# Holding score runs at the head of a query block for the 64-row key tile

## The chip, the cores and the metric

The kernel runs on one core of a Trainium2 chip. The metric is the device time of one execution in microseconds (us). Ten executions of the kernel before were timed; their median is 1172.02 us.

## What is computed

For each of 8 batches, with sequence length S = 3008, width 256 and 64 columns in z:

```
scores = (1/S) * z @ z.T
attn   = max(scores, 0) ** 2
x      = u * (attn @ v)
h      = max(x.T @ w_tok1, 0) @ w_tok2          # mixes tokens, 256 inner
y      = x + h.T
out    = y + max(y @ w_ch1, 0) @ w_ch2          # mixes channels, 1536 inner
```

The scores of a batch are symmetric, because both sides are z.

## The kernel before

**Tiles.** The 3008 tokens are cut into 6 query blocks of 512 (the last has 448) and 24 key tiles of 128 rows, four to a group; group g has the tokens of block g. The last key tile has only 64 rows. Batches, blocks and groups are counted from 0, and "block (4, 5)" is block 5 of batch 4.

**Scores.** A score unit is two key tiles against one query block. z has 64 columns, so a score matmul uses 64 rows of TensorE's array. z is stored twice, in rows 0 to 63 and 64 to 127, and the two matmuls of a unit (L399) use one half each and run side by side. ScalarE takes the ReLU out of PSUM (L437, L425), VectorE squares in place (L445, L473). From batch 1 on only blocks with g >= q are scored. A block g > q is turned by a transposing DMA from SP (`flip`, L492), giving tile `fl`, and serves again as block (g, q). A block with g = q is a triangle tile: only the upper part is scored, and three small transposes on SP (`flip_tiles`, L485) fill in the rest; the first two follow its first unit, the third its second unit. Up to three units are scored in one run, one for each free slot of a ring of three PSUM slots that the mixer also uses.

**Attention times v.** For each query block, six groups of key tiles are multiplied with v into two accumulators, one for each half of the 256 columns (`av_matmul`, L533). These matmuls use 128 rows. The last key tile has 64 rows; its two matmuls, one for each accumulator and again one on each half of the array, are the pair that `do_tails` issues (L533, shown as 64*128). The pair needs the block of the last group (LAST = 5) to be ready and both accumulators to be free. The accumulators become free when VectorE has multiplied the previous block's by u (`gate`, L628 and L633). For query block 5 the block of the last group is the triangle tile (5, 5).

**Mixer.** When a batch's attention is done, its token and channel matmuls (L675, L692, L729, L771, all with 128 rows) are put in two lists, from which pieces are taken between the attention matmuls of the next batch. The transposes of x (L640) and of the sum (L708) and the output's stores (L788, L804) are issued by SP too, as are those of u (L189) and z (L126). GpSimd (POOL) issues the loads of z, v and u (L113, L168, L171, L179), each attached to a step of the attention groups.

**Order.** The kernel writes its own order of instructions, by a planner that runs while the kernel is built. It keeps a clock `pe[0]` for TensorE, estimated times at which engines and tiles are ready, and adds 0.095 us whenever TensorE goes between 64-row and 128-row matmuls (`on_pe`). In each step it picks "scores" (a run of score units), "av" (half a group of attention times v) or "mixer" (a piece of the mixer). `n_now` is the number of units that could be scored at once, `ts` the time when their slots are free, `whole` says that a full run is at hand, `lead` is the number of attention tiles that are alive and `low` that these are at most 3. `blk` is the current query block: `blk.slot` counts the groups it has begun, `blk.tails` says that its pair is issued. `tails_ready` is the time when the pair can be issued. A score run takes the pair along when it can be issued by then; otherwise the pair is issued at the latest before the block's last group:

```python
        if pick == "scores":
            if blk is not None and tails_ready(blk) <= t + 0.3:
                do_tails(blk, max(t, tails_ready(blk)))
            score_run(units[done_units:done_units + n_now], max(pe[0], ts))
```

```python
            if final and not blk.tails:
                do_tails(blk, max(start, tails_ready(blk)))
```

Of the kernel before, what the change touches and what calls it, by code (L numbers as in the profile page):

```python
# [53 lines left out]
def kernel(  # L54
# [12 lines left out]
    B, S, D = u.shape  # L67
# [9 lines left out]
    NQ = (S + QW - 1) // QW  # L77
    NG = KT // GK
# [74 lines left out]
    def fill(n, tag="ps", bufs=3):  # L153

        wp = psum.tile([P, QW], F32, tag=tag, name="wp", bufs=bufs)
        for _ in range(n):
            nc.tensor.matmul(
                wp[:], zero[:, :P], zero[:], start=True, stop=True, skip_group_check=True)
# [94 lines left out]
    LAST = NG - 1  # L253
# [40 lines left out]
    FAR = 1e9  # L294
# [11 lines left out]
    def next_op():  # L306
        best = None
        for e, ops in waiting.items():
            for op in ops:
                if has_room(op.room):  # L310
                    key = (max(free[e], op.ready), -op.first, op.ready)
                    if best is None or key < best[0]:
                        best = (key, e, op)
        return best

    def run_engines(until):

        while True:
            best = next_op()
            if best is None or best[0][0] > until:  # L320
                return
            (start, _, _), e, op = best
            waiting[e].remove(op)
            extra = shared(start, op.busy) - op.busy if e == "sp" else 0.0
            free[e] = start + op.busy + extra
            op.done.t = start + op.lat + extra
            op.fn(op.done.t)

    def known(*events):
        return max((FAR if d.t is None else d.t for d in events), default=0.0)  # L330
# [38 lines left out]
    def can_score(first_unit, most):  # L369

        n, at = 0, live["at"]
        for (b, q, g), pr in units[first_unit:first_unit + most]:
            if (b, q) not in turned or (b, g) not in turned:
                break
            at += pr == 0
            if at > ROOM["at"]:
                break
            n += 1
        return n
# [165 lines left out]
    def block_ready(blk, g):  # L545
        e = blocks.get((blk.b, blk.q, g))
        return FAR if e is None else known(e[0])

    def tails_ready(blk):

        if blk.tails:
            return FAR
        return max(block_ready(blk, LAST), known(*acc_free))

    def do_tails(blk, start):
        on_pe(start, "half", column_time(blk.W))
        blk.parts.setdefault(LAST, 2)
        for dh in range(DT):
            av_matmul(blk, LAST, GK - 1, dh, False)
        blk.tails = True  # L560
        finished(blk, LAST)

    def next_half(t):

        blk = cur[0]
        if blk is None:
            return FAR, None
        if blk.g is not None:
            dh, tiles = blk.steps[blk.half]
            events = early.get((blk.b, blk.q, blk.g), [])[tiles[0]:tiles[-1] + 1]  # L570
            return max(t, known(acc_free[dh], *events)), blk.g
        at = max(t, known(acc_free[0]))
        ready = [(block_ready(blk, g), i) for i, g in enumerate(blk.todo)]
        soon = [i for r, i in ready if r <= at + 0.05]
        if soon:
            return at, blk.todo[soon[0]]
        r, i = min(ready)
        return max(at, r), blk.todo[i]
# [275 lines left out]
    def next_piece(t):  # L854

        best = FAR, None
        slots = [d.t for d in ring if d.t is not None]
        if opened[0] is not None:
            lists = [opened[0]] + [l for l in (heads, tails) if l is not opened[0]]
        else:  # L860
            lists = [heads, tails]
        for l in lists:
            if not l:
                continue
            p = l[0]
            if p.opens and not p.closes and opened[0] is not None:
                continue
            r = max(t, known(*p.needs))
            if p.room and not has_room(p.room):
                r = FAR  # L870
            if not p.closes:
                r = max(r, min(slots)) if slots else FAR
            if r < FAR and r <= t + 0.05:
                return r, l
            if r < best[0]:
                best = r, l
        return best

    def do_piece(start, l):
        p = l.pop(0)  # L880
        start, end = on_pe(start, "full", p.cost)
        opened[0] = l if p.opens else None if p.closes else opened[0]
        p.fn(end)
# [114 lines left out]
    NOW = 0.05  # L998
    STARVED = 0.7
    while cur[0] is not None or heads or tails:  # L1000
        run_engines(pe[0])
        t = pe[0]
        ta, g = next_half(t)
        tm, pieces = next_piece(t)
        blk = cur[0]

        def has_turned(us):
            return known(*(turned[b, c] for (b, q, g_), _ in us for c in (q, g_)))


        n = can_score(done_units, RING)
        slots = sorted(d.t for d in ring if d.t is not None)
        n_now = min(n, len(slots))
        ts = FAR
        if n_now:
            at = max(t, has_turned(units[done_units:done_units + n_now]))
            ts = max([at] + [slots[i] - 0.1 - 0.216 * i for i in range(n_now)])
            new = sum(pr == 0 for _, pr in units[done_units:done_units + n_now])
            if new:
                ts = max(ts, sorted(at_free)[new - 1] - 0.6)  # L1020
        lead = live["at"]
        whole = n_now == RING or (n_now and done_units + n_now == len(units))
        low = lead <= 3
        hold = n >= RING and lead <= 4


        now = sum(d <= t + NOW for d in slots[:n_now])
        left = sum(op.busy for op in waiting["act"])
        starved = blk is not None and blk.b + blk.q == 0 and (
            max(free["act"], t) + left < t + STARVED)  # L1030

        pick = None
        if n_now and ts <= t + NOW and (whole or (low and n_now >= 2)):
            pick = "scores"
        elif (starved and now and can_score(done_units, now) == now
              and has_turned(units[done_units:done_units + now]) <= t + NOW):
            pick, n_now, ts = "scores", now, t
        elif hold and opened[0] is not None and tm <= t + NOW and pieces is opened[0]:
            pick = "mixer"
        elif hold and ta <= t + NOW:  # L1040
            pick = "av"
        elif budget > 0 and tm <= t + NOW:
            pick = "mixer"
        elif ta <= t + NOW:
            pick = "av"
        elif tm <= t + NOW and (budget > -5.0 or blk is None):
            pick = "mixer"
        else:
            options = [(ta, "av"), (tm, "mixer")]
            if n_now and (whole or low):  # L1050
                options.append((ts, "scores"))
            when, what = min(options)
            op = next_op()
            if op is not None and op[0][0] <= when:
                run_engines(op[0][0])
                continue
            assert when < FAR, "nothing can run"
            if blk is not None and blk.b == 0 and blk.q == 0 and blk.acc[1] is None:
                idle = int((when - t) / 0.22)
                if idle:  # L1060
                    fill(idle, "acc1", 1)
            pick = what
# [5 lines that stand above are left out]
            done_units += n_now  # L1068
        elif pick == "av":
            step = (blk.b * NQ + blk.q) * NG + blk.slot  # L1070
            if blk.g is None:
                for f in fetch.get(step, []):
                    f()
            do_half(ta, g)
        else:
            budget -= pieces[0].cost
            do_piece(tm, pieces)
        if pick != "mixer" and blk is not None and blk.b >= 1:
            budget += per_batch * (pe[0] - t) / flat
# [31 lines left out]
```

## Time and profile before

| what | value |
|---|---|
| median of ten executions | 1172.02 us (1170.40 to 1180.49) |
| the profiled execution: its time, its span | 1180.49 us, 1178.4 us |
| TensorE matmuls (PE): busy, instructions | 1162.4 us, 7049 |
| VectorE (DVE), ScalarE (ACT), GpSimd (POOL): busy | 541.6, 521.5, 161.0 us |
| score matmuls L399: instructions | 732 |
| pairs of the 64-row key tile, L533 | 48 pairs |
| transposes L485 into `at`: issues, median to landing | 123, 2.4 us |
| transposes L492 into `fl`: issues, median to landing | 105, 4.0 us |
| DMA engines: mean rate | 141 GB/s |

The profile is of one execution on the chip. A time is counted from the start of the span. "PE" is TensorE's matmuls and "PEld" its weight loads, which overlap. A matmul's busy time goes on after the next one has started, so the time that a matmul costs is read from start to start. A line "X <- Y" among the waits gives the idle time of X that ended with Y, then how often and the longest. "SPq" is SP's queue of issues; for a DMA the time from issue to landing is given apart.

### The profile page before, as it was taken

To read this page: it belongs to the slowest core of one execution; us is meant where nothing else is said; L and a number is where in the kernel's file an instruction comes from. 1 tells how busy PE (TensorE), PEld (TensorE's weight loads), DVE (VectorE), ACT (ScalarE), POOL (GpSimd) and SP (SyncE) were. 2 spreads that over 40 slices of the span, in tenths; PEclk is the share of its full clock that TensorE was granted. 3 is DMA by queue.
4 is the path that set the end of the run, shared out by engine and by line. 5 is a ranking of instruction groups with operands and counts; after the bars stand their busy time and mean duration, and the time that the engine had idled before them with its cause. 6 is when DMAs were issued, how large, how long until landed. Compare 5 with 4: busy or idle time off the path is not lost.

```text
span 1178.4 us, 17791 instructions
## 1 busy us (share of the span) xinstructions
PE 1162.4 (99%) x7049; PEld 630.7 (54%) x7049; DVE 541.6 (46%) x819; ACT 521.5 (44%) x650; POOL 161.0 (14%) x328
## 2 busy tenths in 40 slices
PE   9997999999999999999999999999999999999998
PEld 3332455655556555465555555555554655555666
DVE  5684643436523464334634354342552436512544
ACT  7885542343633355334533436345353445513221
POOL 3471001012011110110201210011101010000000
PEclk9998999999999999999999999999999999999999
DMA  9999836896578984797859896697677978632121
GB/s 167 186 132 185 160 91 149 174 169 123 137 149 167 166 152 115 142 180 146 162 111 184 153 155 136 125 191 140 126 144 143 190 137 155 126 94 63 50 81 63
DMA packets 472883, 165.57 MB, mean 141 GB/s; under 512 B 436640, under 2 KB 450528, under 8 KB 472800
## 3 DMA queue, kind: packets, MB, share of 16 engines
q1 hardware_dynamic: 444944, 131.74, 54.2%
q0 software_dynamic: 27344, 32.32, 19.6%
q8 instruction: 55, 0.90, 0.3%
q10 hardware_dynamic: 512, 0.38, 0.1%
q14 instruction: 28, 0.23, 0.1%
HBM read 65.40 MB, written 24.64 MB: 76 GB/s over the span
## 4 chain that ended last, share of the span: by engine, by line
PE 95%; DMA 2%; DVE 1%; ACT 1%; issue 0%; POOL 0%; SPq 0%; ACTq 0%; DVEq 0%
PE acc L533 40%; PE op L771 21%; PE hp L729 21%; PE sc L399 6%; PE a_ps L675 4%; PE h_ps L692 3%; DMA fl<-at 1%; DMA ur<-in_u_dram 1%; ACT at L437 1%; DMA uT<-ur 0%; DMA zf<-in_z_dram 0%; DVE xT L698 0%; POOL v_sb L168 0%; DVE xT L628 0%; SPq L640 0%
## 5 line engine op out<-in xcount | busy, mean ns | idle before, releaser
L533 PEld LDWEIGHTS <-v_sb 128*128 128x128 bf16 (+1 forms) x2304 | 209.4, 98 | 267.3 <-issue 65.4
L533 PE MATMUL acc<-at,v_sb 128*128 128x512 bf16 (+3 forms) x1464 | 351.1, 379 | 1.3 <-DVE xT L628 0.7
L742 ACT ACTIVATE h2pre<-hp 128x1024 bf16<-128x1024 f32 (+1 forms) x191 | 191.1, 1006 | 364.4 <-PE hp L729 363.3
L437 ACT ACTIVATE at<-sc 128x1024 bf16<-128x1024 f32 (+1 forms) x284 | 271.9, 1023 | 167.6 <-PE sc L399 155.3
L445 DVE TENSOR_TENSOR at<-at 128x1024 bf16<-128x1024 bf16 (+1 forms) x284 | 200.5, 715 | 184.6 <-ACT at L437 184.3
L729 PE MATMUL hp<-xT,w_ch_sb 128*128 128x512 bf16 (+1 forms) x1152 | 266.7, 375 | 0.0
L771 PE MATMUL op<-w_ch_sb,h2pre 128*128 128x256 bf16 x2208 | 258.4, 273 | 0.3 <-DVE xT L698 0.2
L771 PEld LDWEIGHTS <-h2pre 128*128 128x128 bf16 x2208 | 216.0, 98 | 46.1 <-issue 0.5
L533 PE MATMUL acc<-fl,v_sb 128*128 128x512 bf16 (+1 forms) x840 | 199.9, 371 | 0.0
L729 PEld LDWEIGHTS <-w_ch_sb 128*128 128x128 bf16 x1152 | 112.7, 98 | 126.7 <-issue 0.2
L784 DVE TENSOR_TENSOR res<-op,u_sb 128x512 f32<-128x512 f32 x87 | 60.2, 692 | 206.4 <-PE op L771 206.4
L744 DVE TENSOR_SCALAR h2pre<-hp 128x1024 bf16<-128x1024 f32 (+1 forms) x97 | 117.3, 1209 | 52.1 <-PE hp L729 51.1
L628 DVE TENSOR_TENSOR xT<-acc,uT 128x512 bf16<-128x512 f32 (+1 forms) x96 | 63.3, 665 | 114.0 <-PE acc L533 113.6
L399 PE MATMUL sc<-zT 64*128 64x512 bf16 (+1 forms) x732 | 95.6, 361 | 0.5 <-ACT zT L986 0.2
L425 ACT ACTIVATE at<-sc 128x512 bf16<-128x512 f32 (+3 forms) x164 | 59.2, 445 | 67.7 <-PE sc L399 67.5
L125 POOL COPY zr<-zs 128x512 bf16<-128x512 bf16 x42 | 27.2, 648 | 400.7 <-DMA zT<-zr 395.6
L473 DVE TENSOR_TENSOR at<-at 128x512 bf16<-128x512 bf16 (+3 forms) x164 | 44.3, 324 | 59.1 <-ACT at L425 59.1
L399 PEld LDWEIGHTS <-zT 64*128 64x128 bf16 x732 | 31.3, 94 | 57.0 <-issue 40.1
L698 DVE TENSOR_TENSOR xT<-xT,h_ps 128x1024 bf16<-128x1024 bf16 (+1 forms) x48 | 55.7, 1192 | 6.3 <-PE h_ps L692 6.3
L675 PE MATMUL a_ps<-x_sb,w_tok_sb 128*128 128x256 bf16 x384 | 47.1, 281 | 7.6 <-ACT at L437 7.6
L675 PEld LDWEIGHTS <-w_tok_sb 128*128 128x128 bf16 x384 | 38.6, 101 | 17.1 <-issue 8.7
L168 POOL DMA_DIRECT2D v_sb<-in_v_dram x48 | 26.0, 547 | 145.1 <-PE acc L533 143.8
(43 smaller groups left out, 217.3 us busy)
## 6 DMA issues: line engine op xcount, KB each, us to landing
out_dram<-res SPq DMA_DIRECT2D x87, 256.0 KB, 2.2
v_sb<-in_v_dram POOLq DMA_DIRECT2D x40, 256.0 KB, 5.2
ur<-in_u_dram POOLq DMA_DIRECT2D x40, 256.0 KB, 5.4
zs<-in_z_dram POOLq DMA_DIRECT2D x35, 64.0 KB, 5.0
at<-at SPq DMA_TRANSPOSE x123, 2.4
fl<-at SPq DMA_TRANSPOSE x105, 4.0
v_sb<-in_v_dram POOLq DMA_DIRECT2D x8, 192.0 KB, 6.4
ur<-in_u_dram POOLq DMA_DIRECT2D x8, 192.0 KB, 5.7
```

Source lines behind the costliest of these rows:

```text
L399: nc.tensor.matmul(sc[:, r, c0:c1], zT[h, k * P:(k + 1) * P], zT[h, q * QW + c0:q * QW + c1], start=True, stop=True)
L425: nc.scalar.activation(a3[:, i, c0:c1], sc[:, r, c0:c1], ACT.Relu, scale=inv_S)
L437: nc.scalar.activation(view, sv, ACT.Relu, scale=inv_S)
L445: nc.vector.tensor_mul(view, view, view)
L533: nc.tensor.matmul(o, vs[blk.b, g][rows, i, dh * P:(dh + 1) * P], rhs, start=first, stop=stop, skip_group_check=True)
L628: nc.vector.tensor_mul(xT[:, dh, :full * P].rearrange("p (t s) -> p t s", s=P), acc[:, :full * P].rearrange("p (t s) -> p t s", s=P), uT[: ...
L675: nc.tensor.matmul(st["a_ps"][:, th, :], w_tok1_sb[:, k, th * P:(th + 1) * P], x[:, :, i, :], start=(k == 0 and th == 0), stop=(k == KT - ...
L729: nc.tensor.matmul(hp[:, r, :W], w_ch1_sb[:, dc, cc * P:(cc + 1) * P], xT[:, dc, :W], start=(dc == 0), stop=(dc == DT - 1))
L742: nc.scalar.activation(h2[:, :, :W], hp[:, :, :W], ACT.Relu)
L744: nc.vector.tensor_single_scalar(h2[:, :, :W], hp[:, :, :W], 0.0, AX.max)
L771: nc.tensor.matmul(op[:, i, :], h2, w_ch2_sb[:, cc, :], start=(cc == 0 and (i == 0 or apart)), stop=(cc == CHT - 1), skip_group_check=True)
L784: nc.vector.tensor_add(res.rearrange("p i (h d) -> p i h d", d=P), op.rearrange("p i (h d) -> p i h d", d=P), us[:, :, half * 2:half * 2 + ...
```

## The change

A condition `together` is added ahead of the choice, and a score run is not picked by the first rule while it holds. It can hold only in query blocks from 2 on and in batches before the last. It has two cases. In the first, the block has begun no group, its pair is not issued and can't be within 0.3 us, but the block of the last group is already planned. In the second, the current block is block 4, its pair is issued, it is in its last group, and more than three attention tiles are alive. While the condition holds, the planner picks attention or mixer work by its other rules.

```diff
         pick = None
-        if n_now and ts <= t + NOW and (whole or (low and n_now >= 2)):
+        together = blk is not None and blk.q > 1 and blk.b < B - 1 and (
+            not blk.tails and blk.slot == 0 and tails_ready(blk) > t + 0.3
+            and block_ready(blk, LAST) < FAR
+            or blk.tails and blk.q == NQ - 2 and blk.slot >= NG and lead > 3)
+        if n_now and not together and ts <= t + NOW and (whole or (low and n_now >= 2)):
             pick = "scores"
```

`block_ready` is the time when a block of attention is ready, and FAR if it isn't planned yet; NQ and NG are 6. Nothing else in the kernel is changed.

## The prediction

> **What bounds the kernel now.** The page first: busy time by engine, then the chain that ended last.
>
> ```profile
> PE 1162.4 (99%) x7049; PEld 630.7 (54%) x7049; DVE 541.6 (46%) x819; ACT 521.5 (44%) x650; POOL 161.0 (14%) x328
> PE 95%; DMA 2%; DVE 1%; ACT 1%; issue 0%; POOL 0%; SPq 0%; ACTq 0%; DVEq 0%
> ```
>
> TensorE is busy 99% and carries 95% of the chain; nothing else comes near. Its row of waits says how much of its time is waiting:
>
> ```profile
> PE a_ps L675 <- ACT at L437: 7.6, 1, 7.6
> ```
>
> That one wait, at 104.8 us, is nearly all of it; the same view over 200 to 1100 us is empty. So where the change acts, an edit counts only if it alters the time from one matmul to the next, or creates a wait. The timeline of TensorE shows that time (start, busy time, rows, shape, count):
>
> ```profile
> 337.67 1.67 PE L533 MATMUL acc<-fl,v_sb 128*128 128x512 bf16 x7
> 339.28 0.39 PE L533 MATMUL acc<-at,v_sb 64*128 64x512 bf16 x2
> 339.60 1.90 PE L533 MATMUL acc<-fl,v_sb 128*128 128x512 bf16 x8
> 341.34 1.03 PE L729 MATMUL hp<-xT,w_ch_sb 128*128 128x512 bf16 x4
> ```
>
> Read the starts, not the busy times, which overlap. Eight matmuls take 341.34 − 339.60 = 1.74, so 0.216 each with rounding. Seven should end at 337.67 + 1.51 = 339.18; the 64-row pair starts at 339.28, 0.10 late. The pair takes 0.32 to the next matmul, while two 64-row matmuls on opposite halves of the array run together for 0.223. So entering 64-row work costs about 0.10 and leaving it about 0.09: **0.19 per visit**, with no engine waited for. A pair that rides with scores pays neither:
>
> ```profile
> 625.00 0.39 PE L533 MATMUL acc<-at,v_sb 64*128 64x512 bf16 x2
> 625.22 0.43 PE L399 MATMUL sc<-zT 64*128 64x128 bf16 x4
> ```
>
> Here the scores follow 0.22 after the pair.
>
> [...] the clock granted between 104.5 and 125 us is 0.75.
>
> **The change part by part.** In the two built programs the order of TensorE's instructions is the same up to the score run at 211.1 us; the counts (7049 matmuls) are the same throughout. Nothing is added or removed; runs are regrouped.
>
> *Visits removed.* The program before has 140 stretches of 64-row matmuls, 13 of them a lone pair; the changed one has 131, with 4 lone pairs. Ten lone pairs go (in blocks 3 and 5 of several batches, both counted from 0), one comes (block 5 of batch 4). Net 9 × 0.19 = **−1.7 us**. It is on the path: TensorE does not wait there. The pair itself costs 0.22 in either place.
>
> *Score runs held.* They start later, behind attention or mixer matmuls already in the plan. Behind them wait, on ScalarE the ReLU (L425, L437), on VectorE the square (L473, L445), on SP the transposes (L485, L492). ScalarE and VectorE are busy 44% and 46%, so they catch up; TensorE works meanwhile on tiles already made. I cost this at nothing while such tiles last. If they run out, or its score slots are late, TensorE waits: at the turn from block to block I found no such wait before. Around the last batch the order shifts too: TensorE waits there 0.2 (L771 at 1107.79, for VectorE) and may wait once more: 0 to 0.4, taken as 0.
>
> *POOL and SP.* Loads are issued by POOL at steps of the attention groups, so they move with groups. SP issues the same transposes in a changed order. No queue gains an instruction: 0, unless a transpose becomes late.
>
> *A transpose that becomes urgent.* The pair of block 5 reads the last key tile, there a triangle tile completed by L485 transposes. Before, that pair came at the end of block 5, over 17 us after landing in every batch from 1 on. Now it comes at the head. From the pair of block 4 to that of block 5 the changed order leaves, in batches 5 and 6, 34 matmuls of 512 columns and 4 of 448 (34 × 0.216 + 4 × 0.189 = 8.1) and two 64-row stretches (about 0.8 each with their changes): 9.8 us. In that time the second half of the triangle tile must be scored, squared, transposed. On SP its last transpose stands behind x_sb and zT. Nothing before shows this wait; the nearest case is batch 4, whose last transpose also comes this late:
>
> ```profile
> 628.07 1.18 SPq L485 DMA_TRANSPOSE at<-at  x1
> DMA to landing us min/median/max: 5.5/5.5/5.5
> ```
>
> It lands at 633.6, that is 8.6 after the block-4 pair at 625.00. It would fit in 9.8. But the same turn is the time of the loads. The DMA view for 323 to 332 us, no loads, and then for 911 to 916.5, the turn to batch 7:
>
> ```profile
> q1 hardware_dynamic: 4204, 1.25, 56.4%
> x_sb<-xT SPq DMA_TRANSPOSE x1, 2.7
> at<-at SPq DMA_TRANSPOSE x3, 2.3
> ```
>
> ```profile
> q0 software_dynamic: 296, 0.54, 88.4%
> q1 hardware_dynamic: 828, 0.20, 42.9%
> x_sb<-xT SPq DMA_TRANSPOSE x1, 11.2
> at<-at SPq DMA_TRANSPOSE x1, 9.1
> ```
>
> Columns of q: packets, MB, share. With POOL's queue (q0) at 88%, SP's queue (q1) moves 828 packets in 5.5 us against 4204 in 9, and a 2.3 us transpose takes 9.1. SP issues it here:
>
> ```profile
> 914.30 7.08 SPq L485 DMA_TRANSPOSE at<-at  x3
> ```
>
> So it lands at 923.4, which is 13.4 after the block-4 pair at 910.0. Lateness per place is thus from 8.6 − 9.8 < 0, so nothing, to 13.4 − 9.8 = 3.6. A gain is excluded, for the pair had slack before. I take **1.5** at each of the two places, below the middle since one of the two observed ends gives nothing: +3.0. Batch 1 has 13.8 us between its pairs, and there the transposes landed at 211.8 against a pair at 198.9, 12.9: 0 to 0.5, taken as 0. Batches 2 and 3 have over 20 us from scoring the tile to the pair: 0.
>
> *Sum.* −1.7 + 3.0 = **+1.3**. The profiled execution took 1180.49 (span 1178.4, about 2.1 around it); it is the slowest of ten, with the wait at 104.8 that lies ahead of the change. Its sum is 1181.8. The median, 1172.02, differs by that early part, which the change leaves alone, so the same +1.3 gives **1173.3**.
>
> **The rivals.** *Slower: the late triangle tile decides.* Both places lose the full 3.6, batch 1 adds 0.5: 7.7 − 1.7 = +6.0, **1178.0**; a halved clock after a wait could add 1 or 2. It decides once these waits exceed 1.7 + 3.5 = 5.2 together. For it: the load bursts recur at each turn. Against: batch 4's 8.6, and x_sb lands at 2.7 when loads come a little later.
>
> *Faster: the wait that goes is another one.* The next batch's scores stand close to their transposes before: a zT transpose issued at 910.15 lands 4.8 later, 915.0, and the score run that follows starts at 916.10, 1.1 behind. At 346.5 plus 5.8 against 353.1 it is 0.8. In executions where these land later, TensorE waits; the median is 1.6 over the lowest (1170.4). Held scores give them time. If the triangle tile is in time as well: −1.7 − 1.6 = −3.3, and with the loss of an average execution, perhaps 2.5 in place of 1.6, −4.2, **1167.8**. Against: no such wait in the profiled execution.
>
> *The change does nothing:* the held runs cost what the visits save, 1172.0. The order of instructions speaks against that, since nine visits are gone.
>
> **How the numbers follow.** A measurement of this kernel can tell about 0.3%, 3.5 us, from no change. Small net effect (1169 to 1175.5, the visits and part of the waits, the do-nothing case within): 0.42, predicted time 1173.3. Slower rival: 0.36. Faster rival: 0.22. The likeliest case alone covers 1168.5 to 1175.5; since cases of both signs hold most of the chance, the range runs from 1167.3 to 1179.0, leaving out about one in ten at each end: the two full waits with a long halved clock above, both gains at once below.
>
> **What would show it.** Right: nine fewer stretches of 64-row matmuls, each 0.19; a wait "PE acc L533 <- DMA at<-at" at the turns of batches 5 and 6, none in 2 and 3; the transposes just ahead of it at 5 to 10 us to landing. Wrong: no DMA wait on TensorE after 200 us (then −1.7 alone, 1170.3), a wait over 4 us there or a granted clock below 1 after it (slower), or new waits of scores L399 for ScalarE, which would mean that held scores starve the planner's slots.

## The result, and the profile after

The changed kernel takes **1185.1 us** (median of 9 runs, 1183.12 to 1191.47) against 1171.52 us for the kernel before, timed on the same chip (32 runs). The ratio is 1.0105, with a 95% interval of 1.0082 to 1.0127: slower by about 1%, or 13.6 us. The prediction was 1173.3 us with a range to 1179.0, so the result lies outside it, on the slow side.

The page after first, busy time by engine and then the chain that ended last.

```profile
PE 1161.4 (98%) x7049; PEld 630.6 (53%) x7049; DVE 552.0 (47%) x827; ACT 514.1 (43%) x642; POOL 160.8 (14%) x328
PE 93%; DMA 3%; DVE 2%; ACT 1%; issue 1%; SPq 0%; POOL 0%; ACTq 0%; DVEq 0%
```

TensorE still does the same 7049 matmuls, and no other engine has become the bound. But its share of the chain went from 95% to 93%, and that of transfers from 2% to 3%. TensorE's view of waits says which transfer (columns: total us, times, longest):

```profile
PE acc L533 <- DMA at<-at: 10.7, 2, 5.7
PE acc L533 <- DVE xT L628: 2.3, 3, 1.2
...
PE a_ps L675 <- ACT at L437: 0.5, 1, 0.5
```

The first line is new: two waits of over 5 us for a transpose into an attention tile. The third matters for comparing the two profiles. In the kernel before this wait, at 104.8 us, was 7.6 us; it lies ahead of the change. So I compare both traces from matmul 1101, the first that differs, to the last: 962.68 us before, 975.67 us after, **+12.99**.

The timeline of TensorE at the first of the two places (start, busy time, rows, shape, count, idle time before and what ended it):

```profile
755.84 0.39 PE L533 MATMUL acc<-at,v_sb 64*128 64x512 bf16 x2
...
764.75 0.92 PE L533 MATMUL acc<-fl,v_sb 128*128 128x448 bf16 x4
770.71 0.56 PE L533 MATMUL acc<-at,v_sb 64*128 64x448 bf16 x2 [5.04 <-DMA at<-at]
771.03 1.51 PE L399 MATMUL sc<-zT 64*128 64x512 bf16 x6
772.48 1.67 PE L533 MATMUL acc<-fl,v_sb 128*128 128x448 bf16 x4
```

The pair of block (5, 4) starts at 755.84 and that of block (5, 5) at 770.71. The matmuls between them need 9.76 us, so the second pair could have started at 765.60 and waited 5.11. (In e10 below, where this pair waits for nothing, 9.76 is the distance in both batches. The profile counts only 5.04 as idle, since the busy time of the matmul before runs on.) Note the busy time of the last line: four 448-column matmuls take 1.67 us here, 0.92 ahead of the wait. At batch 6 the two pairs are at 902.50 and 918.00, which makes 5.74:

```profile
902.50 0.39 PE L533 MATMUL acc<-at,v_sb 64*128 64x512 bf16 x2
...
918.00 0.55 PE L533 MATMUL acc<-at,v_sb 64*128 64x448 bf16 x2 [5.67 <-DMA at<-at]
```

The view by stretches, with the granted clock (PEclk) as the third column from the end, for the 4 us after each wait:

```profile
770.50:774.50 4.00, 3.79 (x15) 1.37 (x15) 1.39 (x2) 2.77 (x3) 0.05 (x1) 0.57 1.13 246
917.80:922.00 4.20, 4.00 (x17) 1.45 (x18) 1.48 (x3) 2.86 (x3) 0.52 (x1) 0.64 1.20 253
```

TensorE runs at a mean of 0.57 and 0.64 of its clock there. From the start of the pair to that of the fourth group after it takes 4.14 and 3.89 us, against 2.58 for the same matmuls at a clock of 1.00 (in e2 below): 1.56 and 1.31 us more. What TensorE waits for is seen on SP's timeline (here the duration is the issue alone) and in the view of the tile (the last line gives the time from issue to landing):

```profile
758.48 1.26 SPq L640 DMA_TRANSPOSE x_sb<-xT  x1
759.83 1.62 SPq L126 DMA_TRANSPOSE zT<-zr  x1
761.54 6.08 SPq L485 DMA_TRANSPOSE at<-at  x4
```
```profile
L485 SPq DMA_TRANSPOSE at<-at x2: 1194/1712/2230, 761.5 to 762.8; - x2
...
  PE acc L533: 5.0, 1
...
DMA to landing us min/median/max: 8.2/8.6/9.1
```

The third transpose of the triangle tile is issued at 761.54 behind x_sb and zT, and takes 9.1 us to land. At batch 6 it is issued at 908.65 and takes 9.3. The same line's median over the whole kernel is 2.4.

**Accounting for the +12.99.** The two waits give 5.11 + 5.74 = 10.85; the slow clock after them 1.56 + 1.31 = 2.87; the nine visits saved −1.7, which is the prediction's figure and not a measurement of its own. The rest are small gaps in the changed order, from start to start of matmuls: 0.28 at 239.2, a turn from block to block, 0.38 within a score run at 695.9, and 0.47 more than before in the last batch near 1110. That is 1.13. The sum is 10.85 + 2.87 − 1.7 + 1.13 = 13.15, 0.16 above.

### The profile page after: what moved, and what is told of

The parts are those of the page before. It is cut to its first block, busy times and chain, and to the rows that moved or that the text cites. A ratio compares the mean times of both kernels' runs of the same rounds, so it can differ in the third digit from the quotient of the medians.

```text
span 1183.2 us, 17800 instructions
## 1 busy us (share of the span) xinstructions
PE 1161.4 (98%) x7049; PEld 630.6 (53%) x7049; DVE 552.0 (47%) x827; ACT 514.1 (43%) x642; POOL 160.8 (14%) x328
## 4 chain that ended last, share of the span: by engine, by line
PE 93%; DMA 3%; DVE 2%; ACT 1%; issue 1%; SPq 0%; POOL 0%; ACTq 0%; DVEq 0%
PE acc L533 39%; PE op L771 21%; PE hp L729 20%; PE sc L399 6%; PE a_ps L675 3%; PE h_ps L692 3%; DMA at<-at 2%; ACT at L437 1%; DVE at L445 1%; DMA fl<-at 0%; DMA zf<-in_z_dram 0%; DMA v_sb<-in_v_dram 0%; DVE xT L698 0%; DVE xT L628 0%; DVE res L801 0%
## 5 line engine op out<-in xcount | busy, mean ns | idle before, releaser
L533 PE MATMUL acc<-at,v_sb 128*128 128x512 bf16 (+2 forms) x1464 | 348.9, 379 | 13.8 <-DMA at<-at 10.7
L533 PEld LDWEIGHTS <-v_sb 128*128 128x128 bf16 (+1 forms) x2304 | 210.6, 98 | 284.7 <-issue 72.7
L742 ACT ACTIVATE h2pre<-hp 128x1024 bf16<-128x1024 f32 (+1 forms) x183 | 183.7, 1008 | 339.1 <-PE hp L729 334.9
L533 PE MATMUL acc<-fl,v_sb 128*128 128x512 bf16 (+1 forms) x840 | 198.9, 372 | 0.0
L744 DVE TENSOR_SCALAR h2pre<-hp 128x1024 bf16<-128x1024 f32 (+1 forms) x105 | 126.5, 1205 | 60.8 <-PE hp L729 60.0
L675 PE MATMUL a_ps<-x_sb,w_tok_sb 128*128 128x256 bf16 x384 | 44.4, 273 | 0.5 <-ACT at L437 0.5
L692 PE MATMUL h_ps<-w_tok_sb,a_sb 128*128 128x512 bf16 (+1 forms) x192 | 44.7, 375 | 0.1
```

Of the source, the lines that this page charges most:

```text
L533: nc.tensor.matmul(o, vs[blk.b, g][rows, i, dh * P:(dh + 1) * P], rhs, start=first, stop=stop, skip_group_check=True)
L675: nc.tensor.matmul(st["a_ps"][:, th, :], w_tok1_sb[:, k, th * P:(th + 1) * P], x[:, :, i, :], start=(k == 0 and th == 0), stop=(k == KT - ...
L692: nc.tensor.matmul(h[:, dh, :W], st["a"][:, th, dh * P:(dh + 1) * P], w_tok2_sb[:, th, q * QW:q * QW + W], start=(th == 0), stop=(th == 1))
L742: nc.scalar.activation(h2[:, :, :W], hp[:, :, :W], ACT.Relu)
L744: nc.vector.tensor_single_scalar(h2[:, :, :W], hp[:, :, :W], 0.0, AX.max)
```

## The experiments

Theory A: the late triangle tile in batches 5 and 6, with the clock after the wait, is the whole loss. Theory B: holding score runs costs time everywhere, and the two waits only show where it comes due. Theory C, on a part of A: the slow clock is a cost of its own, which goes when TensorE isn't idle. Then come two questions on why the transfer is late: what stands ahead of it on SP, or the loads beside it.

**e1_skip: no holding around block 5 of batches 5 and 6**

```diff
-        together = blk is not None and blk.q > 1 and blk.b < B - 1 and (
+        together = blk is not None and blk.q > 1 and blk.b < B - 1 and not (
+            blk.b in (5, 6) and blk.q >= NQ - 2) and (
```

> The changed kernel, with the hold ruled out in blocks 4 and 5 of batches 5 and 6 alone; all other holds stay, 133 stretches of 64-row matmuls (before 140, changed 131). Theory A, the late triangle tile at two turns: both DMA waits on TensorE (5.1 and 5.7 us in the changed kernel's profile) and the slow matmuls after them go; time 1171.5 - 7 x 0.19 = 1170.2, no wait of TensorE for a DMA after 200 us. Rival B, held scores cost wherever they are held: most of the 13.6 us stays, over 1180.

Measured: 1172.51 us (12 runs), ratio 1.0009 [0.9977, 1.0042]. TensorE waits for no transfer after 200 us. From matmul 1101 it takes 962.52, that is 13.15 less than the change. The transposes of the two tiles are as slow as before (9.2 and 9.5 us to landing), but the pair comes 25 us later. So all that the change lost, it lost at these two places: A, not B. The expected 1170.2 was too low by 2.3. The interval covers that, and the account of the saved visits below explains 1.1 of it.

**e3_plan12: let the planner know that the transpose is late**

```diff
-        done = push("sp", t, 0.3, 5.5, lambda t: blocks.update(
+        done = push("sp", t, 0.3, 12.0 if q == NQ - 1 and b else 5.5, lambda t: blocks.update(
```

> The changed kernel, with the planner told that the third transpose of block 5's triangle tile takes 12.0 us instead of 5.5 (batches from 1 on). It then issues the pair later in batches 1, 5 and 6: 134 stretches of 64-row matmuls. Theory A: no DMA wait on TensorE after 200 us, time 1171.5 - 6 x 0.19 = 1170.4. Rival B, held scores cost: the holds last as long or longer, so 1180 or more.

Measured: 1171.33 us (12 runs), ratio 0.9998 [0.9974, 1.0022]; 962.54 from matmul 1101. TensorE's waits over 200 to 1180 us:

```profile
PE hp L729 <- DVE xT L698: 0.4, 2, 0.2
PE sc L399 <- DVE res L801: 0.2, 1, 0.2
```

No transfer is left. The transposes still take 8.1 and 8.8 us. The planner's figure of 5.5 us let it put the pair where it did; with 12 it moves the pair behind other work, and the loss is gone.

*Where the saved visits went.* e1 has 133 stretches of 64-row matmuls and e3 134, in place of 140: 7 × 0.19 = 1.3 and 6 × 0.19 = 1.1 saved. Yet from matmul 1101 they are only 0.16 and 0.14 faster than the kernel before. The gaps of the change are there too: in e1 0.28 at 239.0, 0.38 at 695.7 and 0.47 in the last batch, 1.13 in all; in e3 0.17, 0.38 and 0.47, 1.02. So the regrouped order saves 1.1 to 1.3 and gives back 1.0 to 1.1.

**e4_warm: 24 matmuls into an accumulator not yet in use, ahead of each of the two late pairs**

```diff
+        if (blk.b, blk.q) in ((5, NQ - 1), (6, NQ - 1)) and blk.acc[1] is None:
+            wp = psum.tile([P, QW], F32, tag="acc1", name="wp", bufs=1)
+            for _ in range(24):
+                nc.tensor.matmul(wp[:], ident[:], w_ch1_sb[:, 0, :QW], ...)
```

> The changed kernel with 24 needless matmuls of 512 columns (5.2 us of work, into the accumulator that the pair then overwrites) ahead of the pair in block 5 of batches 5 and 6, where TensorE otherwise waits 5.1 and 5.7. Theory C, part of the loss is the clock that falls while TensorE idles: the wait is filled, the matmuls after it run at 0.216, and about 1.9 per place is saved, 1185.1 - 3.7 = 1181.4. Rival D, the matmuls after the wait are slow for another cause (the DMA burst): they stay slow, 1185.

Measured: 1182.29 us (10 runs), ratio 1.0091 [1.0058, 1.0123], 2.8 us under the change. The same stretch as above:

```profile
770.50:774.50 4.00, 4.00 (x28) 2.14 (x25) 2.02 (x3) 3.52 (x4) 0.57 (x1) 1.00 1.38 207
```

28 matmuls begin in 4 us in place of 15, at a clock of 1.00 in place of 0.57 (at batch 6, over 917.8 to 922, 1.00 in place of 0.64), although the pair is about as late as in the change: 15.05 and 14.94 us after the pair of block 4, against 14.87 and 15.50. In batch 5 the transpose landed as late as there (9.3 us after its issue); in batch 6 it landed 12.3 us after the pair of block 4, and the added matmuls filled the time up to the pair. C holds: in batch 5 the transfer is as late as in the change and the clock stays at 1.00, so the slow clock comes from the idleness, not from the late transfer as such. The medians alone hardly tell 2.8 us, since the two intervals overlap; from matmul 1101 the trace takes 972.50 with the 48 added matmuls, 3.17 less than the change. Of this 0.38 comes from where the two pairs start, which leaves about 2.8 for the clock; 3.7 was expected.

**e2_vbuf7: seven buffers for v instead of eight**

One load of v then waits longer for its buffer and falls out of the burst of loads at the batch turn: in batch 5 the second group of v is issued at 767.47, when the tile has landed (765.25). The order on every engine is the change's.

```diff
-            vt = sb.tile([P, GK, D], BF16, tag="v", name="v_sb", bufs=8)
+            vt = sb.tile([P, GK, D], BF16, tag="v", name="v_sb", bufs=7)
```

> The changed kernel, order untouched, with 7 buffers for the tiles of v in place of 8, so that one of two loads of v in the burst at the turn of a batch waits until block 5 has used a tile. Theory A1, the transposes are late because the burst of loads thins them out: the third L485 transpose of tiles (5,5) and (6,5) lands in 3 to 6 us instead of 9.1 and 9.3, the waits fall under 1 us each, time 1169.9 to 1172. Rival A2, the tile is late because its last transpose stands behind x_sb and zT in SP's queue, loads or not: waits of over 3 us stay, time over 1180. If the later load of v itself is missed, a wait of L533 or L399 for v_sb shows instead.

Measured: 1175.61 us (20 runs), ratio 1.0030 [1.0007, 1.0054]. The third transposes take 5.4 and 5.8 us, and TensorE waits:

```profile
PE acc L533 <- DMA at<-at: 3.1, 2, 2.4
```

The DMA view of 758 to 771 us, first of the change, then of this kernel, whose trace runs 1.1 us ahead here (packets, MB, share of 16 engines):

```profile
q1 hardware_dynamic: 4077, 0.99, 71.2%
q0 software_dynamic: 592, 0.79, 51.0%
```
```profile
q1 hardware_dynamic: 5243, 1.27, 55.1%
q0 software_dynamic: 465, 0.66, 39.9%
```

POOL's queue q0 moves 0.13 MB less, and SP's queue q1 1166 packets more in 13 us. Each share is of time taken, so q1 needed less time for more packets: share × 16 engines × 13 us, divided by the packets, is 36 ns a packet in the change and 22 here, at 0.24 KB a packet in both. Why q1's packets take longer with one load more is not shown. The waits of 7.7 us less and the clock's 2.9 leave 1185.1 − 10.6 = 1174.5 us, 1.1 under the measured median. So the loads are a large part of the lateness (A1), but not all of it: one wait stayed at 2.38, above the 1 us that A1 allowed, and the time above its 1172.

**e6_x_behind: x_sb behind the third transpose on SP in batches 5 and 6**

```diff
+        def third(t):
+            blocks[b, q, g] = (done, flip_tiles(a3, 2), "at", [1])
+            if kept and q == NQ - 1:
+                turn_x(b, 3, x_done[b, 3].t)
+                kept.clear()
...
```

Block 3's x_sb is held in `kept` until then; only SP's order differs from the change. (Lines move by 5 here, L538 is the former L533.)

> The changed kernel with one difference: on SP the x_sb transpose (L640) of block 3 in batches 5 and 6 is issued just after the third transpose of tile (5,5) or (6,5), not ahead of it and of a zT. All other engines' orders are the same. Theory A3, [...] what stands ahead of the tile counts: it lands 2 to 4 us sooner, waits of 1 to 3.5 in place of 5.1 and 5.7; about 1178. Rival A4, only the end of the load burst counts: the tile still lands when the burst ends, waits of 5 to 6 stay; 1185.

Measured: 1180.46 us (20 runs), ratio 1.0066 [1.0046, 1.0086].

```profile
PE acc L538 <- DMA at<-at: 7.1, 2, 4.1
```

The third transposes are issued 3.8 and 4.7 us after the pair of block 4, in the change 5.7 and 6.15: 1.9 and 1.45 earlier. They still take 8.9 and 9.2 to landing, and the waits shrink only from 5.11 and 5.74 to 2.95 and 4.15. So what stands ahead on SP is worth 2.2 and 1.6 us, and the loads, by e2, 4.4 and 3.4. A3 was right in kind, but one wait and the time stayed above its figures. The stretches after the two waits also show the clock:

```profile
768.20:772.20 4.00, 3.94 (x26) 2.05 (x27) 1.82 (x3) 3.32 (x4) 0.57 (x1) 1.00 0.99 157
912.30:916.50 4.20, 3.87 (x13) 1.32 (x15) 1.52 (x3) 2.85 (x3) 0.31 (x1) 0.50 1.01 225
```

After 2.95 us of waiting the clock is at 1.00, after 4.15 at 0.50.

**e10_xbehind_vbuf7: both remedies on the transfer, TensorE's order as in the change**

> The change with both remedies on the transfer alone: x_sb behind the third transpose on SP in batches 5 and 6, and seven buffers for v; the order of TensorE's work stays that of the change. If what stands ahead on SP (worth about 2 us per place) and the load burst (worth about 4 per place) are separate shares of the 9.2 us, the transpose lands in 4 us or less, no wait of acc on DMA at over 1 us is left, and the time is 1170 to 1173 us. Rival: both edits take away the same time, and the transpose still takes over 5 us: waits of 2 to 3 us stay and the time is 1174 to 1177.

Measured: 1172.43 us (22 runs), ratio 1.0013 [0.9993, 1.0032]; 962.84 from matmul 1101, 12.8 less than the change. TensorE's waits over 200 to 1180 us:

```profile
PE a_ps L686 <- DMA x_sb<-xT: 0.8, 1, 0.8
PE hp L740 <- DVE xT L709: 0.4, 2, 0.2
PE sc L399 <- DVE res L812: 0.2, 1, 0.2
```

No wait of the pair is left, with all nine visits saved. The third transposes now take 5.1 and 4.9 us, not the 4 or less that was expected, but they are issued earlier too. When they land, in us after the pair of block 4 (in e10 the pair that needs them comes at 9.76):

| kernel | batch 5 | batch 6 |
|---|---|---|
| the change | 14.8 | 15.4 |
| e2, seven buffers | 10.5 | 12.2 |
| e6, x_sb behind | 12.7 | 13.9 |
| e10, both | 9.0 | 9.6 |

The shares of e2 and e6 sum to 6.4 and 4.8, and e10 takes off 5.9 in both batches: roughly separate, not exactly. A new wait of 0.8 for x_sb is the price of issuing it later. This run is the clearest proof that the late transfer and its clock, and nothing in TensorE's order, made the change slow. It also shows the ceiling of the change: with the tile in time it is no faster than the kernel before.

**e5_one_place: the condition in batches 5 and 6 only, on the order of the kernel before**

```diff
-        together = blk is not None and blk.q > 1 and blk.b < B - 1 and (
+        together = blk is not None and blk.q >= NQ - 2 and blk.b in (5, 6) and (
```

> The kernel before with the hold allowed only in blocks 4 and 5 of batches 5 and 6. In the built order this moves the pair of block 5 to its head in both, but only in batch 5 is the triangle tile's second half scored just ahead; in batch 6 it is some 25 us old. 138 stretches. Theory A: one DMA wait of about 5 us with about 1.5 us of slow matmuls after it, in batch 5 alone, -2 x 0.19: 1171.5 + 6.1 = 1177.6. Rival B, the hold itself costs: two places lose, or the loss is spread, and it does not follow the one late tile.

Measured: 1174.90 us (20 runs), ratio 1.0017 [0.9991, 1.0043]. The profiled run was the fastest, 1170.67 us, and has one wait for the tile, in batch 5 alone as expected:

```profile
750.61 0.39 PE L533 MATMUL acc<-at,v_sb 64*128 64x512 bf16 x2
...
765.96 0.36 PE L533 MATMUL acc<-at,v_sb 64*128 64x448 bf16 x2 [1.48 <-DMA at<-at]
```

A miss in size: the place is right, the wait is 1.5 and not 5. The tile is as late as in the change, 15.3 us after the pair of block 4 against 14.8, though by another way: both its units are scored behind that pair (750.83), so all three transposes come late (the third at 763.19), and the third takes 2.7 us. But in this order the matmuls between the two pairs take 13.9 us, not 9.76, and so hide most of it. The median is 4.2 us above the profiled run, and the interval includes no change; what the other runs waited for is not seen.

**e8_first_case: the condition without its second case** (the line with `blk.slot >= NG and lead > 3` taken out)

> The changed kernel with the first case of the condition alone (hold at the head of a block until the pair is ready), without the second (hold in the last group of block 4). 135 stretches. In the built order the triangle tiles of batches 5 and 6 are over 20 us old when the pair comes. Theory A: no DMA wait in batches 5 and 6; 1171.5 - 5 x 0.19 = 1170.6. Rival B, the holds at the head cost: over 1175.

Measured: 1171.74 us (20 runs), ratio 0.9994 [0.9975, 1.0014], with 135 stretches and no wait for the tile. So the late pair needs the second case. It does not move the scores of the triangle tile, which follow the pair of block 4 by 0.22 us in both kernels. It keeps back the score run after the next: in e8 that run goes into block 4's last groups (762.47, 902.62), before the tile is there, and the pair comes some 39 us after that of block 4; in the change it is left until block 5's first half group is done, and takes the pair along (770.71, 918.00). The second case alone was not run.

**Fewer buffers for v as a remedy: e7_before_vbuf7, e9_plan12_vbuf7, e11_vbuf6, e12_before_vbuf6**

The edit is the one of e2, with 7 or 6, made in the kernel before (e7, e12), in e3 (e9) and in the change (e11).

> The kernel before with 7 buffers for the tiles of v in place of 8: the control for the run with 7 buffers in the changed kernel. Theory: nothing waits for the later load, 1171 to 1172.5, so that what was left there over 1170 is the two shorter waits of the pair. Rival: the later load costs by itself, 1173 or more, with waits of TensorE for v_sb or for scores.

> The change with the planned latency of a batch's third transpose at 12 us and with seven buffers for v instead of eight. My theory: the planned latency keeps the pair of tile 5 behind the other score runs in batches 5 and 6 (no wait on the transpose, 1171.3 us with that edit alone), and seven buffers take about 1 us off whatever the order is (the kernel before with seven buffers read 1171.1). So about 1170.5 us, 1 to 1.5 us under the kernel before, and no wait of acc on DMA at over 0.5 us after 200 us. Rival: the seventh buffer's gain was only the kernel before's own (its loads land later against other work), or the two edits collide: 1171.5 to 1173.

> The change with six buffers for v instead of eight, the orders of all engines as in the change. If the burst of loads at the turn is what thins the transposes, taking another load of v out of it goes on as the step from eight to seven did (waits 10.7 to 3.1 us): waits of acc on the transposes at 0 to 1.5 us in all, and a time of 1171 to 1174 us. Rival: with six buffers the load of a group waits for its last use in the batch before, so the loads only shift into the time of the transposes or come too late for the next batch's first groups; then a wait of acc on v_sb shows, 1 to 3 us per batch turn in seven turns, and the time is over 1178 us.

> The kernel before with six buffers for v. It measures what the later loads cost by themselves. If the cost is nothing, as with seven buffers (ratio 0.997), 1170 to 1172 us. If the loads come too late for the first groups of the next batch, waits of acc on v_sb of 1 to 3 us at each of seven turns, 1178 us or more.

| kernel | median us (runs) | ratio to before, interval |
|---|---|---|
| e7: before, 7 buffers | 1171.12 (20) | 0.9969 [0.9947, 0.9991] |
| e9: e3, 7 buffers | 1172.21 (22) | 1.0003 [0.9983, 1.0023] |
| e12: before, 6 buffers | 1173.86 (6) | 1.0022 [0.9991, 1.0054] |
| e11: the change, 6 buffers | 1179.47 (6) | 1.0060 [1.0027, 1.0094] |

The later loads of e7 cost nothing, so e2 is not a mixture of a gain and a loss. e9 was meant to beat both kernels and did not: its expected 1170.5 was a miss, and the rival holds. Only e7 is under the kernel before, by 0.3%, and its trace shows no gain: from the pair of block (1, 4) to the last matmul the kernel before, e7 and e12 all take 974.86 us. By these traces the later loads of e12 cost nothing either, though its median lies between its two expectations.

e11 met neither theory whole. Its third transposes of the two tiles take 2.3 us each, no wait of the pair on them is left, and no new wait on v_sb came either (0.6 in the whole trace, 0.5 in the kernel before). But now another transfer is late. The first line is from TensorE's waits, the second from the view by stretches:

```profile
PE a_ps L675 <- DMA x_sb<-xT: 3.5, 1, 3.5
```
```profile
956.50:960.50 4.00, 3.76 (x16) 1.62 (x17) 0.00 (x0) 0.77 (x2) 0.00 (x0) 0.61 0.74 170
```

x_sb took 9.6 us to land just ahead of 957, the mixer waited 3.5 us for it, and the clock fell to 0.61. From 944 to 957 POOL's queue moves 0.96 MB; that the moved loads of v delay x_sb is likely, but no run separates it. The profiled run is the fastest of six (1175.28); what the others waited for is not seen, so the median's further 4 us stay open.

## Why the prediction was wrong

*Bound and method.* Right. TensorE set the time, and each part of the result is a time from one matmul to the next or a wait.

*Visits removed, −1.7.* Right as far as the runs can tell: with it the account of the trace closes within 0.2 us.

*Held scores at nothing, the last batch 0 to 0.4 taken as 0.* Too small by 1.13: 0.28 at a turn from block to block, 0.38 inside a score run, 0.47 in the last batch. This is why the change without its late tile gains nothing (e1, e3, e10). The rival "the change does nothing" is what remains once that tile is in time, though it was meant for the whole.

*A transpose that becomes urgent, +1.5 at each of two places.* **The step that failed.** Place, cause and direction were right: batches 5 and 6, none in 2 and 3, nothing in batch 1 (the tile landed 0.9 us ahead of its pair). The distance between the pairs was right too, 9.8 against 9.76. The arrival was not. Predicted was 8.6 to 13.4 after the pair of block 4; measured is 14.8 (770.67 − 755.84) and 15.4 (917.95 − 902.50). Of the far end, the 9.1 us to landing was right (9.1 and 9.3), but the issue came 5.7 and 6.15 us after that pair, not 4.3. The far end was read from another tile: by the order of the score units, the transposes at 914.30 are those of block (7, 0), while tile (6, 5) had landed at 895.1 in the kernel before. The issue was not late because of the scores. In the change they follow the pair at once (two of the six matmuls of the first line are the tile's second unit):

```profile
756.06 0.54 PE L399 MATMUL sc<-zT 64*128 64x128 bf16 x6
...
757.19 1.19 SPq L126 DMA_TRANSPOSE zT<-zr  x1
```

The tile's last square ends at 757.44, and SP issues the transpose 4.1 us later, behind a row of zT, x_sb and zT. That row begins 1.35 and 1.90 us after the pair of block 4, at the far end 0.15 (910.15 against 910.00). So the wait is 5.1 and 5.7, above the stated 3.6. And the middle was no fair choice between the ends: the near one, batch 4's 5.5 us, was a transpose ahead of the loads of v, which POOL issued from 634.10 on, when it had landed (633.6); in the change they are issued from 758.32 on, ahead of the transpose. The prediction itself saw the burst at each turn. One of the two ends described the place, the other didn't. The trace before also held a later landing that the prediction passed over: in batch 5 itself the third transpose, issued at 775.08 with both units scored behind block 4's pair, landed 15.6 us after that pair (777.64 against 762.01).

*The clock.* Left out of the sum and put at "1 or 2" in the slower rival, an estimate that names no source; measured 2.9 over both places. It could have been bounded. The trace before has the halved clock, after its wait of 7.57 us that ended at 112.75:

```profile
112.00:118.00 6.00, 4.86 (x20) 2.20 (x20) 3.49 (x6) 3.89 (x5) 1.47 (x4) 0.50 1.11 251
118.00:122.00 4.00, 4.00 (x28) 3.17 (x27) 1.41 (x2) 0.57 (x1) 2.60 (x5) 0.72 1.20 165
```

A mean of 0.72 over the second stretch is 0.50 until about 120.2, so 7.5 us of half clock follow the wait; as an estimate from that trace, a place could cost up to half of these, 3.7 us. In the change the clock is at 0.50 for a shorter time, from 770.6 to 774.0 and from 917.4 to 920.8. Of that, 3.3 and 2.8 us follow the waits, and half of these, 1.7 and 1.4, is near the measured 1.56 and 1.31. Over the runs, waits of 0.73, 2.38 and 2.95 us left the clock at 1.00; 3.5, 4.15, 5.04 and 5.67 brought it to 0.61, 0.50, 0.57 and 0.64 over the next 4 us. They show no one length of wait at which it falls: in the change's two it was still at 1.00 over the first 4.9 us.

*The rivals.* The slower one named the mechanism and its point: it decides once the waits exceed 5.2 together. They came to 10.85. Its price of 6.0 was half of the measured 13, for the two reasons above. Its two signs, a wait over 4 us and a granted clock below 1 after it, both came. The faster rival fell: after 200 us no trace has a score run that waits over 0.2 us for zT, and e10, with the tile in time, isn't faster than the kernel before.

## What to carry to other kernels

When a change moves a consumer up to its producer, take the duration of the producer's transfer from the same stage of the profile, with the loads that run there, and its issue from the new order; a middle between a busy and a quiet stage describes neither. Add the clock to a long TensorE wait: in these runs it was at 1.00 after waits of up to 2.95 us and at 0.50 to 0.64 over the 4 us after waits of 3.5 us and more, which cost 1.56 and 1.31 us at the two places of the change. And a planner's figure for a transfer is a place to look: raising one from 5.5 to 12 us took away the whole loss here (e3).

## What the runs showed of the hardware that was not expected

- The penalty of the clock is separate from the wait: e4's filler matmuls kept the clock at 1.00 in place of 0.57 and 0.64 and took about 2.8 us off, although the pair started about as late.
- A transpose that takes 2.4 us at the median took 9.1 to 9.3 beside a burst of loads. One load of 256 KB less in the burst brought it to 5.4 and 5.8, a further one to 2.3 in both batches (e11).
- The transfer that is late can change with the buffers: in place of the transpose of the tile in the change, e11 has a late x_sb (9.6 us to landing), with a like fall of the clock (0.61).
